# A value from two products, and a gate in one accumulation bank, in the last four blocks of a fused Fourier-mixing and ReGLU kernel

## The chip, the cores and the metric

One core of a Trainium2 chip. The metric is device time in microseconds of one execution of the whole program. A core has five engines with queues of their own: TensorE (PE in the profile, with its weight loads as PEld), VectorE (DVE), ScalarE (ACT), GpSimd (POOL) and SyncE (SP, which issues most transfers). Each takes its instructions in order and waits at each for what other engines must have done.

## The reference

```
X = fft(x, axis=1); X = fft(X, axis=2); y = X.real         # x: 8 x 3008 x 256
out = (max(y @ w_gate, 0) * (y @ w_val)) @ w_out           # weights 256 x 1536, 1536 x 256
```

There are 24064 rows (8 sequences of 3008). Inputs and output are float32; the kernel's products take bfloat16.

## The kernel before

The Fourier transform over the 256 channels is folded into the weights: `WA` holds the cosine-transformed and `WB` the sine-transformed gate (index 0) and value (index 1) weights. The transform over the sequence is done on PE from folded inputs and gives, for each sequence b, a cosine part `U` and a sine part `V`. Row j of the result and its mirror row S - j have the same cosine product and sine products of opposite sign. So a **tile**, which is 128 of the 1536 hidden features (`fi`, 0 to 11) by one **block** of columns (512, 512 or 481: `thirds`), gives two halves of the hidden layer `h`: one from cosine plus sine, one from cosine minus sine. `WM` is -2 times `WB`, with row 0 set to zero; row 0 of `V` carries one channel that has no sine, and its term is seeded into the bank separately: ACT writes `CB` times a column of `b2` into the bank (`seed`, L1011) before the products add to it.

After sequence 0, which is done in another way, there are 7 x 3 x 12 = 252 tiles, and the program makes one call of `slot` for each. A slot works on five tiles at once. For tile `cur` with number fi:

- `nxt` (two ahead): PE makes the sine product of the gate in bank `g` (`sine_part`, L1016), ACT copies it out (L1019); PE adds the cosine product to the seeded bank `p` (`cosine_part`, L1023); DVE forms the sum, `sp` (`both`, L1027), and POOL the difference, `sm` (L1028).
- `after` (three ahead): ACT seeds its bank `p`. There are two such banks.
- `pending` (one behind): PE adds `WM` times `V` to its value bank `v` (`mirror`, L879), which turns cosine plus sine into cosine minus sine; DVE multiplies it by the positive part of `sm` (`relu_mult` in `second`, L909).
- `cur`: PE makes the value's cosine and sine products (`value`, L873 and L874); DVE multiplies by the positive part of `sp` (L909).
- In two places of the slot PE runs `outs` products of 256 columns (L781), the last layer's output of the block before, 5/8 after the sine product and the rest at the end. After 24 of them a bank of output is full; ACT evicts it (L794, one eviction per slot from the list `evict`) and SP sends it to memory (L806).

For a 481-column tile SP also copies the last 66 columns of `h` to `LB` (`keep_rest`, L904). `sums` holds the DVE steps of the sequence's transform; POOL's folding of the next sequences' inputs is dealt out by `run_fold`. Both are done before the last block of sequence 6. The bank `d` belongs to the transform's products. `kvec` is used only for the tables of the transform, while sequence 0 is worked on.

The bank for each output and the order of everything on each engine are those of the program text; no planner moves them.

Of the kernel before, what the change touches and what calls it, by code (L numbers as in the profile page):

```python
# [12 lines left out]
BF16 = mybir.dt.bfloat16  # L13
# [16 lines left out]
def dram(ap, offset, pattern):  # L30
    return bass.AP(ap.tensor, offset, [list(p) for p in pattern])
# [3 lines left out]
def kernel(  # L35
# [27 lines left out]
    def single(name, shape, dt=F32, pool=const):  # L63
        return pool.tile(shape, dt, name=name, tag=name)
# [218 lines left out]
    ums = single("ums", [128, 1])  # L283
    m2 = single("m2", [128, 1])
    half_pi = single("half_pi", [128, 1])
    kvec = single("kvec", [128, NK])
    dvec = single("dvec", [128, 129], pool=st_)
    go = single("go", [128, 2])
    c128p = single("c128p", [128, 2, 3, 2])
# [212 lines left out]
            nc.gpsimd.tensor_tensor(FF[0][p, 0, t, :, 0:1], even[:, :, 0:1], even[:, :, 0:1], op=ALU.add)  # L502
    start_pool.__exit__(None, None, None)
    ch128 = nc.dram_tensor("ch128", (B, 4 * NJ + 1), BF16, kind="Internal").ap()
    b2 = single("b2", [128, NF])
    wrow = nc.dram_tensor("wrow", (1, DF), BF16, kind="Internal").ap()
    brow = single("brow", [128, NF], BF16)


    def even_table(n, c):  # L510
# [321 lines left out]
    for seg in (2, 3):  # L832
        more.setdefault((1, 8 + seg), []).append(lambda seg=seg: minus_v(nc.scalar, seg))

    more[(1, 1)].append(lambda: nc.sync.dma_start(out=wrow, in_=WB[0][0:1, :]))
    more[(1, 4)].append(lambda: nc.sync.dma_start(out=brow[:], in_=dram(wrow, 0, [[1, 128], [128, NF]]), allow_slow_non_contiguous=True))
    more[(2, 2)] = [lambda: nc.scalar.copy(b2[:], brow[:])]
    more_1 = {}
    for at, step in zip((-5, -4, -3, -2, -1, 7, 7, 8, 14, 17), channel_loads() + channel_turn()):
# [16 lines left out]
    def run_one(todo):  # L856
        if todo:
            todo.pop(0)()
# [62 lines left out]
    def value(st):  # L921
        st["v"] = bank("v")
        two(st["v"], st, 1)
# [63 lines left out]

    def new_tiles():  # L990
        for b in range(1, B):
            for blk, block in enumerate(thirds):
                for fi in range(NF):
                    st = tile_of(block, fi, uv[b])
                    st["b"] = b
                    st["kind"] = "o" if (b, blk, fi) == (1, 0, 6) else "n"
                    st["lead"] = (b, blk, fi) == (1, 0, 0)
                    yield st

# [21 lines left out]
    def cosine_part(st):  # L1021
        n = st["n"]
        nc.tensor.matmul(st["p"][:, 0:n], lhsT=WA[0][:, st["f"]], rhs=st["us"], start=False, stop=True, skip_group_check=True)  # L1023

    def both(st):
        n, (q, sp, sm) = st["n"], st["s"]
        nc.vector.scalar_tensor_tensor(sp[:, 0:n], in0=q[:, 0:n], scalar=-0.5, in1=st["p"][:, 0:n], op0=ALU.mult, op1=ALU.add)  # L1027
        nc.gpsimd.tensor_tensor(sm[:, 0:n], sp[:, 0:n], q[:, 0:n], op=ALU.add)  # L1028

    def slot(cur, mid, nxt, after, outs, fold_us):  # L1030

        stop = len(todo_out)

        def out(part):
            run(todo_out, len(todo_out) - stop + outs * part // 8)
        old = nxt is not None and nxt["kind"] == "o"
        new = nxt is not None and not old
# [36 lines left out]
        return cur  # L1074
# [4 lines left out]
    for b in range(B):  # L1079
# [4 lines left out]
        for blk, block in enumerate(blocks):  # L1084
# [44 lines left out]
            if (b, blk) == (0, 0):  # L1129
                for fi in range(NF):  # L1130
                    st = tile_of(block, fi, (U, V, CB))
                    add_h(st, hs)
                    if fi == 8:
                        todo_out = out_steps(b, block, hs, True)
                    pending = first_tile(st, more.get((0, fi), ()), 6)
                mirror(pending["g"], pending, 0)
                relu(pending)
            elif not paired:
                for fi in range(NF):
                    st = tile_of(block, fi, (U, V, CB))  # L1140
                    add_h(st, hs)
                    tag = {(3, 8): "g", (3, 9): "d", (3, 10): "g", (3, 11): "d"}.get((blk, fi), "p")
                    last = []
                    if (blk, fi) == (3, 11):
                        last = [lambda: (sine_part(ahead[1]), cosine_part(ahead[1]), both(ahead[1]), seed(ahead[2]))]
                    if (blk, fi) == (3, 9):
                        ahead = [next(tiles) for _ in range(3)]
                        more[(3, 9)] += [lambda: seed(ahead[0], prime())]
                        more[(3, 10)] += [lambda: seed(ahead[1], prime())]
                        more[(3, 11)] += [lambda: (sine_part(ahead[0]), cosine_part(ahead[0]), both(ahead[0]))]  # L1150
                    if (blk, fi) == (1, 8):
                        run(todo_out, len(todo_out))
                        todo_out = out_steps(b, block, hs, True)
                    pending = single_tile(st, 3 if blk == 1 else per_tile // 2, more_b.get((blk, fi), ()), last, tag)
                    run(todo_dft, DFT_0[blk - 1][fi])
            else:
                for fi in range(NF):
                    at = NF * blk + fi
                    cur = ahead.pop(0)
                    add_h(cur, hs)  # L1160
                    ahead.append(next(tiles, None))
                    outs = per_tile
                    if (b, blk) == (B - 1, 2) and fi > 8:
                        outs = (10, 11, 17)[fi - 9]
# [52 lines left out]
```

## Time and profile before

| | |
|---|---|
| time, median of 3 runs | 629.87 us (629.80 to 630.07) |
| the profiled execution's own time | 629.88 us |
| its span, first to last instruction | 628.1 us |
| DVE, ACT, POOL busy | 88%, 71%, 80% of the span |
| POOL busy in 400 to 450 us, and in 560 to 580 us | 44.66 of 50 us, 13.19 of 20 us |
| granted PE clock | 1.00 |

A line of the groups view reads: source line, engine, operation, output and input by the program's names, shapes, count, then busy time and mean duration, then the engine's idle time ahead of these instructions and what ended most of it. A line of the timeline reads: start in us, duration, engine, line, operation, names, shapes, count of merged instructions, and in brackets the idle time ahead of it with its releaser. A line of the windows view gives a stretch, its length, then busy time and instruction count of PE, PEld, DVE, ACT and POOL, the granted clock, the DMA engines' share and their GB/s. Matmuls are pipelined, and the ends of their rows are modelled.

### The profile page before, as it was taken

What the parts mean: (1) busy time and instruction counts of PE and PEld (TensorE: products, weight loads), DVE (VectorE), ACT (ScalarE), POOL (GpSimd) and SP (SyncE); (2) the same over time, 40 slices, a digit from 0 to 9 for tenths busy, and PEclk for the clock granted to TensorE, in tenths of its full rate; (3) what the DMA queues carried; (4) which work ended last, traced back from release to release, by engine and by line L of the source; (5) the groups of instructions that cost most, each with busy time, mean ns of one, the idle gap of its engine ahead of it and who ended that gap; (6) DMA issues with size and microseconds to landing.
All of it is one profiled execution on the core that took longest, in us unless ns stands there. A gap on an engine that the chain in (4) does not pass through costs nothing.

```text
span 628.1 us, 12374 instructions
## 1 busy us (share of the span) xinstructions
PE 617.9 (98%) x4057; PEld 398.2 (63%) x4102; DVE 550.9 (88%) x979; ACT 445.8 (71%) x814; POOL 502.7 (80%) x478
## 2 busy tenths in 40 slices
PE   8999999999999999999999999999999999999997
PEld 3566666666666666666666666666666666666666
DVE  8886676999899899988999999899999989999991
ACT  7796667777677767777777767777777777777762
POOL 8988992998899988799979989699886566666660
PEclk9999999999999999999999999999999999999999
DMA  9954758734263427315362326211221111211113
GB/s 240 210 201 130 169 184 106 186 66 141 86 155 137 132 70 196 101 48 161 91 185 68 131 76 138 61 52 35 76 62 37 42 60 56 60 35 50 53 50 95
DMA packets 84465, 66.47 MB, mean 106 GB/s; under 512 B 40070, under 2 KB 67494, under 8 KB 84400
## 3 DMA queue, kind: packets, MB, share of 16 engines
q1 hardware_dynamic: 79814, 60.01, 34.5%
q0 software_dynamic: 3984, 4.92, 4.0%
q8 instruction: 32, 0.52, 0.4%
q10 hardware_dynamic: 602, 0.75, 0.3%
q14 instruction: 33, 0.27, 0.1%
HBM read 41.88 MB, written 34.17 MB: 121 GB/s over the span
## 4 chain that ended last, share of the span: by engine, by line
PE 93%; DVE 3%; issue 1%; ACT 1%; DMA 1%; DVEq 0%; ACTq 0%
PE o L781 37%; PE v L874 10%; PE v L879 10%; PE g L1016 8%; PE p L1023 8%; PE v L873 8%; PE d L585 4%; DVE h L909 2%; PE p L879 1%; PE p L873 1%; PE p L874 1%; PE v L395 1%; DMA XG<-in_x_dram 1%; DVE h L898 1%; DVE r L1027 1%
## 5 line engine op out<-in xcount | busy, mean ns | idle before, releaser
L1028 POOL TENSOR_TENSOR r<-r 128x512 f32<-128x512 f32 (+1 forms) x251 | 312.8, 1252 | 100.0 <-DVE r L1027 98.9
L909 DVE SCALAR_TENSOR_TENSOR h<-r,v 128x512 bf16<-128x512 f32 (+1 forms) x502 | 317.3, 673 | 39.1 <-PE v L879 25.5
L781 PE MATMUL o<-wo,h 128*128 128x256 bf16 x2172 | 330.7, 273 | 0.0
L781 PEld LDWEIGHTS <-h 128*128 128x128 bf16 x2220 | 216.4, 97 | 112.7 <-issue 1.6
L1011 ACT ACTIVATE p<-CB,b 128x512 f32<-128x512 bf16 (+1 forms) x251 | 171.7, 684 | 73.5 <-DVE r L1027 72.6
L1019 ACT COPY r<-g 128x512 f32<-128x512 f32 (+1 forms) x251 | 144.8, 577 | 65.4 <-PE g L1016 56.8
L1027 DVE SCALAR_TENSOR_TENSOR r<-r,p 128x512 f32<-128x512 f32 (+1 forms) x251 | 168.1, 670 | 0.6 <-ACT r L1019 0.6
L874 PE MATMUL v<-V,WB 128*128 128x512 bf16 (+3 forms) x296 | 108.7, 367 | 2.2
L879 PE MATMUL v<-V,WM 128*128 128x512 bf16 (+1 forms) x252 | 94.4, 375 | 1.1 <-DVE h L909 0.7
L1016 PE MATMUL g<-V,WM 128*128 128x512 bf16 (+1 forms) x251 | 94.2, 375 | 0.2
L1023 PE MATMUL p<-U,WA 128*128 128x512 bf16 (+1 forms) x251 | 94.2, 375 | 0.0
L873 PE MATMUL v<-U,WA 128*128 128x512 bf16 (+3 forms) x254 | 92.7, 365 | 0.0
L898 DVE TENSOR_TENSOR h<-r,v 128x376 bf16<-128x376 f32 (+2 forms) x90 | 46.0, 546 | 17.3 <-PE v L879 9.1
L873 PEld LDWEIGHTS <-WA 128*128 128x128 bf16 x348 | 33.9, 97 | 39.9 <-issue 10.7
L874 PEld LDWEIGHTS <-WB 128*128 128x128 bf16 x348 | 33.9, 97 | 33.7 <-ACT WB L677 0.2
L794 ACT COPY os<-o 128x512 f32<-128x512 f32 x92 | 52.6, 571 | 3.5 <-issue 3.0
L198 POOL TENSOR_TENSOR XG<-XG,XD 128x510 f32<-128x510 f32 x42 | 52.9, 1267 | 0.6 <-DMA XG<-xr 0.6
L889 ACT ACTIVATE r<-p 128x376 f32<-128x376 f32 (+1 forms) x80 | 38.0, 486 | 17.8 <-PE p L879 9.6
L206 POOL TENSOR_TENSOR AA<-XG 128x510 f32<-128x510 f32 x42 | 45.3, 1089 | 0.0
L1016 PEld LDWEIGHTS <-WM 128*128 128x128 bf16 x251 | 24.5, 98 | 5.7 <-issue 0.3
L879 PEld LDWEIGHTS <-WM 128*128 128x128 bf16 x253 | 24.7, 98 | 3.1
L1023 PEld LDWEIGHTS <-WA 128*128 128x128 bf16 x251 | 24.5, 98 | 3.3 <-issue 0.2
(183 smaller groups left out, 412.4 us busy)
## 6 DMA issues: line engine op xcount, KB each, us to landing
out_dram<-os SPq DMA_DIRECT2D x124, 128.0 KB
xr<-in_x_dram SPq DMA_DIRECT2D x12, 768.0 KB
XG<-xr SPq DMA_DIRECT2D x12, 768.0 KB
XD<-in_x_dram SPq DMA_DIRECT2D x15, 512.0 KB
out_dram<-os SPq DMA_DIRECT2D x35, 112.0 KB
XD<-in_x_dram SPq DMA_DIRECT2D x8, 448.0 KB
CB<-ch SPq DMA_DIRECT2D x7, 376.2 KB
out_dram<-os SPq DMA_DIRECT2D x13, 96.0 KB
```

Of the source, the lines that this page charges most:

```text
L198: e.tensor_tensor(XG[p, r, t, ::-1, 1:D], XG[p, r, t, ::-1, 1:D], XD[p, r, t, :, D - 1:0:-1], op=ALU.add)
L781: nc.tensor.matmul(st["p"][0:m, q, :], lhsT=lhs(f), rhs=wo[:, f, :], start=(f == 0 and not (early and q)), stop=(f == NF - 1), skip_group_ ...
L873: nc.tensor.matmul(bank[:, 0:st["n"]], lhsT=WA[i][:, st["f"]], rhs=st["us"], start=True, stop=False)
L874: nc.tensor.matmul(bank[:, 0:st["n"]], lhsT=WB[i][:, st["f"]], rhs=st["vs"], start=False, stop=True)
L879: nc.tensor.matmul(bank[:, 0:st["n"]], lhsT=W[i][:, st["f"]], rhs=v, start=False, stop=True, skip_group_check=True)
L909: nc.vector.scalar_tensor_tensor(half_h(st, sign), in0=st["s"][1 + sign][:, 0:n], scalar=0.0, in1=st["v"][:, 0:n], op0=ALU.max, op1=ALU.mult)
L1011: nc.scalar.activation(st["p"][:, 0:st["n"]], st["c"], ACTF.Copy, scale=b2[:, st["fi"]:st["fi"] + 1])
L1016: nc.tensor.matmul(st["g"][:, 0:n], lhsT=WM[0][:, st["f"]], rhs=st["vs"], start=True, stop=True)
L1019: nc.scalar.copy(q[:, 0:n], st["g"][:, 0:n])
L1023: nc.tensor.matmul(st["p"][:, 0:n], lhsT=WA[0][:, st["f"]], rhs=st["us"], start=False, stop=True, skip_group_check=True)
L1027: nc.vector.scalar_tensor_tensor(sp[:, 0:n], in0=q[:, 0:n], scalar=-0.5, in1=st["p"][:, 0:n], op0=ALU.mult, op1=ALU.add)
L1028: nc.gpsimd.tensor_tensor(sm[:, 0:n], sp[:, 0:n], q[:, 0:n], op=ALU.add)
```

## The change

In the four last blocks (the third of sequence 6 and all of sequence 7), two kinds of tiles are worked in another way. The block is named by (sequence, third), as in (7, 0).

- Tiles 3 and 8 (`SHORT`): the value's bank is `d`, seeded by ACT two slots ahead. PE adds the cosine product a slot ahead, ACT keeps twice that in SBUF (`a`), POOL takes the positive part of `sm`. In its own slot PE adds one sine product from `WV`, a copy of `WB[1]` with row 0 zero; DVE makes the first half as before, then `a` minus the bank, and POOL multiplies that by `sm` for the second half. The third product (`mirror`) and the second `relu_mult` are gone for these tiles. In `slot`, `both` of a later tile stands ahead of the difference.
- Tile 5 (`JOINED`): the gate has one bank. After the cosine product ACT keeps twice the bank (`sm`); in the next slot PE adds the sine product to the same bank, ACT copies it out as `sp`, and POOL subtracts it from `sm`. `sine_part` and `both` are gone for this tile. The slot in which its cosine product is made takes two more output products and no eviction; the next takes two fewer.
- Once: `WV` is made by three ACT multiplications in sequence 2 in the space of `kvec`; the seeds' table `b2` and its load have 24 columns instead of 12; row 0 of `WB[0]` is overwritten by zeros in sequence 5; one product opens bank `d` at the start of (6, 2).

```diff
-    kvec = single("kvec", [128, NK])
+    kvec = single("kvec", [128, DF // 2])
...
-    b2 = single("b2", [128, NF])
+    b2 = single("b2", [128, 2 * NF])
+    WV = kvec[:].bitcast(BF16)
...
-    more[(1, 1)].append(lambda: nc.sync.dma_start(out=wrow, in_=WB[0][0:1, :]))
-    more[(1, 4)].append(lambda: nc.sync.dma_start(out=brow[:], in_=dram(wrow, 0, [[1, 128], [128, NF]]), ...))
+    more[(1, 1)].append(lambda: [nc.sync.dma_start(out=wrow[i:i + 1], in_=WB[i][0:1, :]) for i in range(2)])
+    more[(1, 4)].append(lambda: nc.sync.dma_start(out=brow[:], in_=dram(wrow, 0, [[1, 128], [128, 2 * NF]]), ...))
...
+    JOINED, SHORT = (5,), (3, 8)
...
+                    late = b == 7 or (b, blk) == (6, 2)
+                    st["kind"] = "o" if (b, blk, fi) == (1, 0, 6) else "j" if late and fi in JOINED else "n"
+                    st["short"] = late and fi in SHORT
...
+    def copy_cosine(st):
+        n, sp, sm = st["n"], space(), space()
+        st["s"] = sm, sp, sm
+        nc.scalar.mul(sm[:, 0:n], st["p"][:, 0:n], 2.0)
+
+    def add_sine(st):
+        n, (_, sp, sm) = st["n"], st["s"]
+        nc.tensor.matmul(st["p"][:, 0:n], lhsT=WB[0][:, st["f"]], rhs=st["vs"], start=False, stop=True, ...)
+        nc.scalar.copy(sp[:, 0:n], st["p"][:, 0:n])
+        nc.gpsimd.tensor_tensor(sm[:, 0:n], sm[:, 0:n], sp[:, 0:n], op=ALU.subtract)
+
+    def open_bank():
+        p = bank("d")
+        nc.tensor.matmul(p[:], lhsT=WA[1][:, 0:128], rhs=U[:, 0:512], start=True, stop=True)
+
+    def seed_value(st):
+        st["v"] = bank("d")
+        nc.scalar.activation(st["v"][:, 0:st["n"]], st["c"], ACTF.Copy, scale=b2[:, NF + st["fi"]:NF + st["fi"] + 1])
+
+    def value_cosine(st):
+        n, st["a"], sm = st["n"], space(), st["s"][2][:, 0:st["n"]]
+        nc.tensor.matmul(st["v"][:, 0:n], lhsT=WA[1][:, st["f"]], rhs=st["us"], start=False, stop=True, ...)
+        nc.scalar.mul(st["a"][:, 0:n], st["v"][:, 0:n], 2.0)
+        nc.gpsimd.tensor_scalar(sm, sm, scalar1=0.0, op0=ALU.max, scalar2=None)
+
+    def value_sine(st):
+        n = st["n"]
+        nc.tensor.matmul(st["v"][:, 0:n], lhsT=WV[:, st["f"]], rhs=st["vs"], start=False, stop=True, ...)
+
+    def value_second(st):
+        n = st["n"]
+        a = st["a"][:, 0:n]
+        nc.vector.tensor_tensor(a, a, st["v"][:, 0:n], op=ALU.subtract)
+        nc.gpsimd.tensor_tensor(half_h(st, 1), st["s"][2][:, 0:n], a, op=ALU.mult)
+        if n == 481:
+            keep_rest(st)
...
     def slot(cur, mid, nxt, after, outs, fold_us):
+        joined, ready = (st is not None and st["kind"] == "j" for st in (nxt, mid))
+        outs += 2 * joined - 2 * ready
...
+        if ready:
+            add_sine(mid)
-        if new and not lead:
+        if (new or joined) and not lead:
             cosine_part(nxt)
+        if joined:
+            copy_cosine(nxt)
         if not lead:
             seed(after)
-        if pending is not None:
+        if mid is not None and mid["short"]:
+            value_cosine(mid)
+        if pending is not None and not pending.get("short"):
             mirror(pending["v"], pending, 1)
-        if pending is not None:
             second(pending)
-        value(cur)
+        if cur["short"]:
+            value_sine(cur)
+        else:
+            value(cur)
...
+        if cur["short"]:
+            value_second(cur)
+        if nxt is not None and nxt["short"]:
+            seed_value(nxt)
         run_fold(fold_us)
-        run_one(evict)
+        if not joined:
+            run_one(evict)
...
+                    if (b, at) in ((2, 5), (2, 9), (2, 13)):
+                        f = slice(128 * (at - 5), 128 * (at - 1))
+                        nc.scalar.mul(WV[:, f], WM[1][:, f], -0.5)
+                    if (b, at) == (5, 0):
+                        nc.sync.dma_start(out=WB[0][0:1, :], in_=WM[0][0:1, :])
+                    if (b, at) == (6, 24):
+                        open_bank()
```

More of the change, by code (lines that the diff above doesn't have):

```diff
@@ L504 @@
     ch128 = nc.dram_tensor("ch128", (B, 4 * NJ + 1), BF16, kind="Internal").ap()
-    b2 = single("b2", [128, NF])
-    wrow = nc.dram_tensor("wrow", (1, DF), BF16, kind="Internal").ap()
-    brow = single("brow", [128, NF], BF16)
+    b2 = single("b2", [128, 2 * NF])
+    WV = kvec[:].bitcast(BF16)
+    wrow = nc.dram_tensor("wrow", (2, DF), BF16, kind="Internal").ap()
+    brow = single("brow", [128, 2 * NF], BF16)
     def even_table(n, c):
@@ L833 @@
         more.setdefault((1, 8 + seg), []).append(lambda seg=seg: minus_v(nc.scalar, seg))
-    more[(1, 1)].append(lambda: nc.sync.dma_start(out=wrow, in_=WB[0][0:1, :]))
-    more[(1, 4)].append(lambda: nc.sync.dma_start(out=brow[:], in_=dram(wrow, 0, [[1, 128], [128, NF]]), allow_slow_non_contiguous=True))
+    more[(1, 1)].append(lambda: [nc.sync.dma_start(out=wrow[i:i + 1], in_=WB[i][0:1, :]) for i in range(2)])
+    more[(1, 4)].append(lambda: nc.sync.dma_start(out=brow[:], in_=dram(wrow, 0, [[1, 128], [128, 2 * NF]]), allow_slow_non_contiguous=True))
     more[(2, 2)] = [lambda: nc.scalar.copy(b2[:], brow[:])]
@@ L995, in new_tiles @@
                     st["b"] = b
-                    st["kind"] = "o" if (b, blk, fi) == (1, 0, 6) else "n"
+                    late = b == 7 or (b, blk) == (6, 2)
+                    st["kind"] = "o" if (b, blk, fi) == (1, 0, 6) else "j" if late and fi in JOINED else "n"
+                    st["short"] = late and fi in SHORT
                     st["lead"] = (b, blk, fi) == (1, 0, 0)
@@ L1028, in both @@
         nc.gpsimd.tensor_tensor(sm[:, 0:n], sp[:, 0:n], q[:, 0:n], op=ALU.add)
+    def copy_cosine(st):
[4 more added lines that the diff above has]
+        n, (_, sp, sm) = st["n"], st["s"]
+        nc.tensor.matmul(st["p"][:, 0:n], lhsT=WB[0][:, st["f"]], rhs=st["vs"], start=False, stop=True, skip_group_check=True)
+        nc.scalar.copy(sp[:, 0:n], st["p"][:, 0:n])
[8 more added lines that the diff above has]
+        n, st["a"], sm = st["n"], space(), st["s"][2][:, 0:st["n"]]
+        nc.tensor.matmul(st["v"][:, 0:n], lhsT=WA[1][:, st["f"]], rhs=st["us"], start=False, stop=True, skip_group_check=True)
+        nc.scalar.mul(st["a"][:, 0:n], st["v"][:, 0:n], 2.0)
+        nc.gpsimd.tensor_scalar(sm, sm, scalar1=0.0, op0=ALU.max, scalar2=None)
+    def value_sine(st):
+        n = st["n"]
+        nc.tensor.matmul(st["v"][:, 0:n], lhsT=WV[:, st["f"]], rhs=st["vs"], start=False, stop=True, skip_group_check=True)
+    def value_second(st):
[5 more added lines that the diff above has]
+            keep_rest(st)
     def slot(cur, mid, nxt, after, outs, fold_us):
+        joined, ready = (st is not None and st["kind"] == "j" for st in (nxt, mid))
+        outs += 2 * joined - 2 * ready
         stop = len(todo_out)
@@ L1036, in slot @@
         old = nxt is not None and nxt["kind"] == "o"
-        new = nxt is not None and not old
+        new = nxt is not None and nxt["kind"] == "n"
         if old:
```

## The prediction, made before the changed kernel ran

> **What bounds the kernel now.** I read the page's span and busy times first, then busy time by stretches of the span, then who waited for whom, then the timeline of one slot, engine by engine. "Slot" is one call of `slot`: one tile's value and one later tile's gate.
>
> ```profile
> span 628.1 us, 12374 instructions
> PE 617.9 (98%) x4057; PEld 398.2 (63%) x4102; DVE 550.9 (88%) x979; ACT 445.8 (71%) x814; POOL 502.7 (80%) x478
> ```
> ```profile
> 560.00:580.00 20.00, 19.85 (x133) 13.03 (x134) 19.30 (x32) 14.23 (x24) 13.19 (x11) 1.00 0.15 48
> ```
>
> PE is busy for 98% of the span, and for 19.85 of 20 us in a stretch inside the last four blocks; DVE, at 19.30, is hardly less loaded. A busy PE alone proves little, since a matmul's row includes its drain. So I asked for PE's waits from 525 to 601 us, nearly all of the stage that changes. The answer is its header, with no row under it:
>
> ```profile
> engine line waited for: us in total, times, longest us
> ```
>
> PE waits for nobody there. What counts then is the distance from one product's start to the next:
>
> ```profile
> 562.01 0.38 PE L1016 MATMUL g<-V,WM 128*128 128x512 bf16 x1
> 562.23 0.71 PE L781 MATMUL o<-wo,h 128*128 128x256 bf16 x5
> 562.77 0.38 PE L1023 MATMUL p<-U,WA 128*128 128x512 bf16 x1
> 562.99 0.38 PE L879 MATMUL v<-V,WM 128*128 128x512 bf16 x1
> 563.20 0.38 PE L873 MATMUL v<-U,WA 128*128 128x512 bf16 x1
> 563.42 0.38 PE L874 MATMUL v<-V,WB 128*128 128x512 bf16 x1
> 563.63 0.49 PE L781 MATMUL o<-wo,h 128*128 128x256 bf16 x3
> 563.96 0.38 PE L1016 MATMUL g<-V,WM 128*128 128x512 bf16 x1
> ```
>
> This is a slot of a 512-column block. It repeats after 563.96 - 562.01 = 1.95 us. Between 562.77 and 563.63 lie four products of 512 columns, (563.63 - 562.77) / 4 = 0.215 us each, though each row lasts 0.38; an output product of 256 columns takes (562.77 - 562.23) / 5 = 0.108. Five times 0.215 and eight times 0.108 make 1.94: the slot is the sum of PE's spacings. The same in a block of 481 columns:
>
> ```profile
> 600.71 0.37 PE L1016 MATMUL g<-V,WM 128*128 128x481 bf16 x1
> 601.46 0.37 PE L1023 MATMUL p<-U,WA 128*128 128x481 bf16 x1
> 601.66 0.37 PE L879 MATMUL v<-V,WM 128*128 128x481 bf16 x1
> 602.07 0.37 PE L874 MATMUL v<-V,WB 128*128 128x481 bf16 x1
> 602.60 0.37 PE L1016 MATMUL g<-V,WM 128*128 128x481 bf16 x1
> ```
>
> The slot is 602.60 - 600.71 = 1.89 us, a product (602.07 - 601.46) / 3 = 0.203.
>
> Now DVE, which could take over:
>
> ```profile
> 562.72 0.68 DVE L1027 SCALAR_TENSOR_TENSOR r<-r,p 128x512 f32<-128x512 f32 x1
> 563.47 1.28 DVE L909 SCALAR_TENSOR_TENSOR h<-r,v 128x512 bf16<-128x512 f32 x2
> 564.68 0.68 DVE L1027 SCALAR_TENSOR_TENSOR r<-r,p 128x512 f32<-128x512 f32 x1
> ```
> ```profile
> 602.14 1.22 DVE L909 SCALAR_TENSOR_TENSOR h<-r,v 128x481 bf16<-128x481 f32 x2
> 603.27 0.65 DVE L1027 SCALAR_TENSOR_TENSOR r<-r,p 128x481 f32<-128x481 f32 x1
> ```
>
> L909 twice and L1027 once are its work in a slot. Two L909 rows last 1.28 together, yet L1027 starts 564.68 - 563.47 = 1.21 after the first: operations start 0.605 apart, (603.27 - 602.14) / 2 = 0.565 at 481 columns. Three of them need 1.815 of 1.95 us. DVE keeps 0.135 us in reserve per slot, and no more.
>
> **The change, part by part.** All of it is set against the profiled execution, 629.88 us (span 628.1 and 1.78 around it), which is 0.01 from the median of the three runs, 629.87.
>
> *PE.* A short tile's value was three products (L873, L874, and L879 in the next slot). It becomes two: the cosine product a slot earlier and a sine product in place of L873 and L874. One product is gone for each short tile. Tiles 3 and 8 of four blocks are eight: four at 0.215 and four at 0.203, 1.67 us. `open_bank` adds one product of 0.215. A joined gate has two products as before; its sine product moves one slot on, and two output products (2 x 0.108) fill the place it leaves, to be missed in the next slot, so PE's sum stays. Net -1.67 + 0.215 = -1.46 us, if PE waits for nothing new. It is not the 0.38 of a row times eight: rows overlap. At one place the Trainium skill differs: the page "TensorE: Matmul & The Clock Gate", section "Back-to-back issue gap", gives about 131 ns per 512-column product in a stream of loads and products. By that the net would be 7 x 0.131 = 0.92; the 0.215 here speaks against it (the same section's 216 ns for an isolated product agrees).
>
> *DVE.* Costs of its new operation and of what the other engines are given come from these groups, or their nearest relatives:
>
> ```profile
> L898 DVE TENSOR_TENSOR h<-r,v 128x512 bf16<-128x512 f32 x2 | 1.4, 684 | 0.3 <-PE v L879 0.3
> L1028 POOL TENSOR_TENSOR r<-r 128x512 f32<-128x512 f32 x167 | 212.0, 1274 | 72.7 <-DVE r L1027 72.0
> L487 POOL TENSOR_SCALAR AA<-AA 128x377 f32<-128x377 f32 x6 | 3.8, 627 | 0.5
> L1011 ACT ACTIVATE p<-CB,b 128x512 f32<-128x512 bf16 x167 | 115.8, 693 | 47.2 <-DVE r L1027 46.2 <-PE v L874 0.6 <-PE p L1003 0.4
> L1019 ACT COPY r<-g 128x512 f32<-128x512 f32 x167 | 97.7, 585 | 47.7 <-PE g L1016 39.3 <-POOL r L1028 6.0 <-POOL AA L206 0.4
> ```
>
> A joined gate takes L1027 off DVE in one slot. For a short tile the second L909 goes and `value_second`'s difference comes; the nearest row is the 512-column TENSOR_TENSOR that also reads PSUM, 684 ns, like L909's 0.68. So per short tile DVE saves nothing, but the work moves a slot ahead. At tile 3 this is free: the same slot has the joined gate, so three operations stay. At tile 8 there are four in one slot: tile 7's second half, tile 8's first half, tile 10's L1027 and the difference. What waits behind the fourth? The next slot's first operation, L909 of tile 9; and behind that PE, because tile 9's third product (L879) adds into the bank that this L909 reads. What such a release costs is seen at the end of the program:
>
> ```profile
> 614.17 1.23 DVE L909 SCALAR_TENSOR_TENSOR h<-r,v 128x481 bf16<-128x481 f32 x2 [1.39 <-PE v L874]
> ```
> ```profile
> 615.45 0.36 PE L879 MATMUL v<-V,WM 128*128 128x481 bf16 x1 [0.58 <-DVE h L909]
> ```
>
> DVE ends at 614.17 + 1.23 = 615.40 and PE starts at 615.45, so 0.05. Counted from the start of tile 8's slot, at 512 columns: L879 issues at 562.99 - 562.01 = 0.98 and DVE starts at 563.47 - 562.01 = 1.46. Four starts 0.605 apart free DVE at 3.88. Tile 9's L909 runs to 3.88 + 0.68 = 4.56, and PE may go on at 4.61. PE, whose slots 8 and 9 are both one product shorter (1.735), wants L879 of tile 9 at 2 x 1.735 + 0.98 = 4.45. It waits 0.16. At 481 columns: 1.43 + 4 x 0.565 = 3.69, with 0.65 and 0.05 4.39, against 2 x 1.687 + 0.95 = 4.32, so 0.07; in the last block slots 9 and 10 carry more output products, and nothing waits. Together 2 x 0.16 + 0.07 = 0.39 us. The bounds: 0 if DVE turns round a little faster than 0.605, and, if each operation held DVE for its full 0.68 (0.65), 4.18 + 0.68 + 0.05 - 4.45 = 0.46 twice and 0.43 once, 1.35. I take 0.39, from spacings seen in this very stage. Net: -1.46 + 0.39 = -1.07.
>
> *ACT.* Its slot, with an eviction in it:
>
> ```profile
> 562.48 0.59 ACT L1019 COPY r<-g 128x512 f32<-128x512 f32 x1 [0.30 <-PE g L1016]
> 563.44 0.69 ACT L1011 ACTIVATE p<-CB,b 128x512 f32<-128x512 bf16 x1 [0.37 <-DVE r L1027]
> 564.07 0.57 ACT L794 COPY os<-o 128x512 f32<-128x512 f32 x1
> 564.55 0.58 ACT L1019 COPY r<-g 128x512 f32<-128x512 f32 x1
> ```
>
> Copies start 564.55 - 564.07 = 0.48 apart, a seed holds ACT for 564.07 - 563.44 = 0.63. A short tile adds a seed (0.63) and a scaled copy (nearest row L1019, 585 ns, so 0.48), a joined gate one copy more. The narrow place is the slot after a joined gate. There `add_sine` issues after one product and three output products, at 0.215 + 3 x 0.108 = 0.54; a product's result reaches ACT 562.48 - 562.01 = 0.47 later, at 1.01; the copy ends at 1.59; the next seed, which needs that bank, starts 0.04 later (L1027 ends at 562.72 + 0.68 = 563.40, the seed starts at 563.44) and ends at 1.63 + 0.69 = 2.32. Its cosine product is due at 1.735 + 0.76 = 2.495 (562.77 - 562.01). The cover is 0.17 us, so the cost is nothing, and every ACT operation that lands ahead of that seed uncovers 0.48 - 0.17 = 0.31. The eviction that would stand there is held back by `if not joined`, to the end of this slot; the output bank it empties is wanted again only two groups of 24 products later.
>
> *POOL.* Per short tile it adds an elementwise maximum (nearest 0.627 for 377 elements, so about 0.85 for 512; between 0.63 and 1.27) and the product for the mirrored half (nearest 1.27). Around tile 8 it has 4 x 1.27 + 0.85 = 5.93 in three slots of 1.95 + 0.215 + 1.735 + 1.735 = 5.64, so it falls 0.3 behind. That is hidden: the product is read by the next block's output products, the sums two slots later. On SP the copy of a 481-column tile's rest waits for POOL now, some 1.3 us longer, and output transfers queue behind it; four output buffers cover that. If they did not, PE would wait up to 1.3 at each of four such tiles, no row points to that.
>
> *Early parts.* `brow` has 3072 elements to fetch, not 1536:
>
> ```profile
> 46.01 0.39 SPq L836 DMA_DIRECT2D brow<-wrow  x1
> ```
> ```profile
> 46.00:50.00 4.00, 4.00 (x29) 2.43 (x27) 3.08 (x8) 3.03 (x8) 0.76 (x2) 1.00 0.91 200
> 50.00:54.00 4.00, 4.00 (x29) 2.38 (x27) 2.17 (x5) 2.57 (x6) 4.00 (x5) 1.00 0.19 62
> ```
> ```profile
> 63.66 0.19 ACT L837 CAST b<-brow 128x12 f32<-128x12 bf16 x1
> ```
>
> The load, issued at 46.01, keeps the DMA engines at 0.91 up to 50 and leaves 0.19 after; as long again would end by 54, and the reader comes at 63.66. It costs nothing; with the cover gone, 4 us at most. The extra row copies are 3 KB each. The three `WV` multiplications (at most the seed's 0.69 each) stand ahead of a slot's copy on ACT in the third sequence:
>
> ```profile
> 188.44 0.58 ACT L794 COPY os<-o 128x512 f32<-128x512 f32 x1
> 188.91 0.58 ACT L1019 COPY r<-g 128x512 f32<-128x512 f32 x1
> 189.86 0.69 ACT L1011 ACTIVATE p<-CB,b 128x512 f32<-128x512 bf16 x1 [0.37 <-DVE r L1027]
> ```
>
> Here an eviction, a copy and a seed follow each other at 188.44, 188.91 and 189.86, with 0.37 idle before the seed; PE wants that seed's bank a further 0.59 after it ends (563.44 + 0.69 = 564.13 against 562.77 + 1.95 = 564.72). 0.37 + 0.59 is more than 0.69: nothing, and 3 x 0.69 = 2.1 if it is uncovered.
>
> **The rivals.**
> *All hidden.* DVE turns round fast enough for tile 9: -1.46, 628.4 us. For it: only 0.16 is missing. Against: the 0.605.
> *DVE takes the gain.* Each operation holds DVE for its full duration: stalls 1.35, net -0.11, 629.8 us. For it: 96% busy. Against: starts 0.605 apart. On the Trainium skill's page "VectorE: DVE Perf Modes", section "The DRAIN you can't avoid", the next operation does not start before the pipe empties unless it is one that is not held; the trace shows the exception.
> *A product frees less than its spacing*, at least the 0.108 of the nearest shorter one: 7 x 0.108 = 0.76, with the stall 629.5 us. For it is only the page's 131 ns; against it the equal spacings.
> *ACT becomes the bound, and the kernel slower.* If the seed and copy for tile 3 (0.63 + 0.48) are still queued when the joined gate's copies come, 1.11 - 0.17 = 0.94 is lost at each of four gates: 629.88 - 1.07 + 3.76 = 632.6 us. It decides from a backlog of 0.17 + 1.07 / 4 = 0.44. For it: three additions fall into slots 1 to 4, 0.63 + 2 x 0.48 = 1.6. Against: ACT idles 0.30 and 0.37 in such slots, 2.7 in four, less one or two evictions.
> *The `WV` work is uncovered*: 628.8 + 2.1 = 630.9 us.
> That the change does not do what it says can't be: the products are counted out in the program.
>
> **How the numbers follow.** Forecast: 629.88 - 1.07 = 628.8 us. Chances: forecast 0.50, all hidden 0.20, DVE 0.12, frees less 0.03, ACT 0.12, `WV` 0.03. A measurement of this kernel tells about 0.2% (1.26 us) from no change. Faster by more needs stalls below 0.2: all hidden, and 0.15 of the forecast's 0.50, together 0.35. Slower is ACT and `WV`, 0.15. Within 0.2% is the rest, 0.50. The range: down to 628.2, all hidden less 0.2 for the scatter of the runs (629.8 to 630.07); up to 630.2, which takes in the DVE case and a part of the ACT backlog, and leaves out ACT in full and `WV`, 0.15.
>
> **What would show it.** L879 should appear 8 times less often. Slots 8 and 9 should last 1.735 and 1.69 us. PE should wait for L909 before tile 9's L879, some 0.16 us in (7, 0) and (7, 1). No PE wait on ACT's seed should appear. A PE row waiting for L1011 at slots 4 and 5 proves the ACT rival; waits of 0.4 and more at tile 9 prove the DVE one; slots 8 and 9 shortened by less than 0.2 without a wait prove the third; a gap on PE near slots 5, 9 and 13 of the third sequence proves `WV`. Late `brow` would show as idle ACT before its copy.

## The result, and the profile after

| | before | after |
|---|---|---|
| median, 14 runs each | 629.88 us (629.59 to 630.53) | 628.42 us (628.22 to 628.99) |
| ratio | | 0.9978 (95% interval 0.997 to 0.9985) |
| span of the profiled execution | 628.1 us | 626.4 us |

1.46 us faster, 0.22%. A second comparison of the same two kernels on another chip gave 629.99 and 628.69 us, ratio 0.998 (0.9971 to 0.9989).

First the page's span and busy times, the stretch from 560 to 580 us, and PE's waits from 515 to 616 us, each of the changed kernel:

```profile
span 626.4 us, 12435 instructions
PE 618.8 (99%) x4095; PEld 397.7 (63%) x4095; DVE 547.7 (87%) x975; ACT 455.6 (73%) x837; POOL 523.4 (84%) x494
```
```profile
560.00:580.00 20.00, 20.00 (x136) 13.10 (x135) 19.01 (x31) 16.16 (x28) 17.76 (x15) 1.00 0.16 49
```
```profile
PE v L880 <- DVE h L910: 0.2, 1, 0.2
```

The columns of the stretch are PE, PEld, DVE, ACT and POOL. DVE fell from 19.30 to 19.01 us in it, ACT rose from 14.23 to 16.16 and POOL from 13.19 to 17.76. PE is full, 20.00. The 19.85 of before was no idle time: in that stretch three products of L873 have a weight load and no row of their own. For the same reason the count of PE's rows grows, from 4057 to 4095, though the weight loads fall from 4102 to 4095: eight products gone and one added. Behind 515 us the third product has 44 rows (L880), where it had 52 (L879). The view of waits knows one wait in the whole stage; waits shorter than a row's overlap with the next (about 0.16 us) do not show in it, so PE has to be read from start to start.

PE in the timeline, the slot of tile 3 in (7, 0), from one L1028 (the cosine product, L1023 before) to the next L1021 (L1016 before):

```profile
550.81 0.38 PE L1028 MATMUL p<-U,WA 128*128 128x512 bf16 x1
551.02 0.38 PE L880 MATMUL v<-V,WM 128*128 128x512 bf16 x1
551.24 0.38 PE L1064 MATMUL d<-V,kvec 128*128 128x512 bf16 x1
551.46 0.60 PE L782 MATMUL o<-wo,h 128*128 128x256 bf16 x4
551.89 0.38 PE L1021 MATMUL g<-V,WM 128*128 128x512 bf16 x1
```

Tile 3's value is the one product L1064, at the spacing of 0.215: this slot lost exactly one product. The slots of tiles 8 and 9 last 1.74 us each, from L1028 to L1028, and 1.69 at 481 columns, where they had 1.95 and 1.89.

Then the wait that was forecast, in (7, 0): DVE in the slot of tile 8, and PE ahead of tile 9's third product (L880):

```profile
561.77 0.68 DVE L910 SCALAR_TENSOR_TENSOR h<-r,d 128x512 bf16<-128x512 f32 x1
562.37 0.68 DVE L1032 SCALAR_TENSOR_TENSOR r<-r,p 128x512 f32<-128x512 f32 x1
562.96 0.68 DVE L1069 TENSOR_TENSOR r<-r,d 128x512 f32<-128x512 f32 x1
563.56 0.68 DVE L910 SCALAR_TENSOR_TENSOR h<-r,v 128x512 bf16<-128x512 f32 x1
```
```profile
563.93 0.38 PE L1028 MATMUL p<-U,WA 128*128 128x512 bf16 x1
564.30 0.38 PE L880 MATMUL v<-V,WM 128*128 128x512 bf16 x1
564.51 0.38 PE L874 MATMUL v<-U,WA 128*128 128x512 bf16 x1
```

Tile 8's first half, tile 10's sum, the difference and tile 9's first half start 0.60, 0.59 and 0.60 apart. The last ends at 563.56 + 0.68 = 564.24; L880 starts at 564.30, where 563.93 + 0.215 = 564.15 would have followed without a wait: 0.15 us.

And the last slot, whose rows of before are in the prediction: PE's products for tiles 10 and 11 (L880), and DVE.

```profile
612.11 0.37 PE L880 MATMUL v<-V,WM 128*128 128x481 bf16 x1
613.86 0.36 PE L880 MATMUL v<-V,WM 128*128 128x481 bf16 x1 [0.21 <-DVE h L910]
```
```profile
612.58 1.23 DVE L910 SCALAR_TENSOR_TENSOR h<-r,v 128x481 bf16<-128x481 f32 x2 [1.02 <-PE v L880]
```

The pair of L910 starts 612.58 - 612.11 = 0.47 us after tile 10's product. In the kernel before, tile 10's product was this row:

```profile
613.33 0.37 PE L879 MATMUL v<-V,WM 128*128 128x481 bf16 x1
```

It started at 613.33 and the pair at 614.17, 0.84 later. So PE now waits 0.37 us less ahead of tile 11's last product, at a place that the change does not touch.

Distances between PE starts, less the spacing of the product in front, give all of PE's waits from 516 to 616 us:

| | before | after |
|---|---|---|
| slot of tile 0 of (6, 2), ahead of L880 (L879 before) | 0.10 | 0 |
| ahead of tile 9's L880 (L879 before), in (6, 2), (7, 0), (7, 1), (7, 2) | 0, 0, 0, 0.05 | 0.05, 0.15, 0.17, 0.16 |
| ahead of tile 11's last product | 0.75 | 0.38 |
| sum | 0.90 | 0.91 |

The eight products, less the one that opens the bank, are 1.67 - 0.215 = 1.46 us. The new waits and the lost ones cancel. From tile 11's cosine product in (6, 1), at 516.55 and 516.43 us, to the end of the span are 111.57 us before and 109.98 after: 1.59 less, of which 0.12 is the landing of the last transfer.

### The profile page after: what moved, and what is told of

It is laid out like the page before. It is cut to its first block, busy times and chain, and to the rows that moved or that the text cites. A ratio compares the mean times of both kernels' runs of the same rounds, so it can differ in the third digit from the quotient of the medians.

```text
span 626.4 us, 12435 instructions
## 1 busy us (share of the span) xinstructions
PE 618.8 (99%) x4095; PEld 397.7 (63%) x4095; DVE 547.7 (87%) x975; ACT 455.6 (73%) x837; POOL 523.4 (84%) x494
## 4 chain that ended last, share of the span: by engine, by line
PE 93%; DVE 3%; ACT 1%; issue 1%; DMA 1%; DVEq 0%; ACTq 0%
PE o L782 37%; PE v L880 10%; PE v L875 9%; PE v L874 9%; PE g L1021 8%; PE p L1028 8%; PE d L586 4%; DVE h L910 2%; PE p L880 1%; PE p L874 1%; PE p L875 1%; PE v L395 1%; DMA XG<-in_x_dram 1%; DVE h L899 1%; DVE r L1032 1%
## 5 line engine op out<-in xcount | busy, mean ns | idle before, releaser
L1033 POOL TENSOR_TENSOR r<-r 128x512 f32<-128x512 f32 (+1 forms) x247 | 308.0, 1254 | 77.7 <-DVE r L1032 76.3
L910 DVE SCALAR_TENSOR_TENSOR h<-r,v 128x512 bf16<-128x512 f32 (+1 forms) x486 | 307.8, 673 | 40.6 <-PE v L880 30.0
L1016 ACT ACTIVATE p<-CB,b 128x512 f32<-128x512 bf16 (+1 forms) x251 | 171.8, 685 | 66.9 <-DVE r L1032 65.2
L1024 ACT COPY r<-g 128x512 f32<-128x512 f32 (+1 forms) x247 | 142.6, 577 | 58.3 <-PE g L1021 49.3
L1032 DVE SCALAR_TENSOR_TENSOR r<-r,p 128x512 f32<-128x512 f32 (+1 forms) x247 | 165.2, 669 | 0.6 <-ACT r L1024 0.6
L875 PE MATMUL v<-V,WB 128*128 128x512 bf16 (+3 forms) x288 | 105.6, 367 | 0.0
L874 PE MATMUL v<-U,WA 128*128 128x512 bf16 (+3 forms) x288 | 105.6, 367 | 0.0
L1028 PE MATMUL p<-U,WA 128*128 128x512 bf16 (+1 forms) x251 | 94.1, 375 | 0.0
L1021 PE MATMUL g<-V,WM 128*128 128x512 bf16 (+1 forms) x247 | 92.6, 375 | 0.2
L880 PE MATMUL v<-V,WM 128*128 128x512 bf16 (+1 forms) x244 | 91.4, 375 | 0.7 <-DVE h L910 0.4
L795 ACT COPY os<-o 128x512 f32<-128x512 f32 x92 | 52.6, 571 | 3.4 <-PE o L782 3.4
L1021 PEld LDWEIGHTS <-WM 128*128 128x128 bf16 x247 | 24.2, 98 | 5.6 <-issue 0.3
L1028 PEld LDWEIGHTS <-WA 128*128 128x128 bf16 x251 | 24.6, 98 | 3.3 <-issue 0.2
L880 PEld LDWEIGHTS <-WM 128*128 128x128 bf16 x245 | 24.0, 98 | 3.8
```

Source lines behind the costliest of these rows:

```text
L874: nc.tensor.matmul(bank[:, 0:st["n"]], lhsT=WA[i][:, st["f"]], rhs=st["us"], start=True, stop=False)
L875: nc.tensor.matmul(bank[:, 0:st["n"]], lhsT=WB[i][:, st["f"]], rhs=st["vs"], start=False, stop=True)
L880: nc.tensor.matmul(bank[:, 0:st["n"]], lhsT=W[i][:, st["f"]], rhs=v, start=False, stop=True, skip_group_check=True)
L910: nc.vector.scalar_tensor_tensor(half_h(st, sign), in0=st["s"][1 + sign][:, 0:n], scalar=0.0, in1=st["v"][:, 0:n], op0=ALU.max, op1=ALU.mult)
L1016: nc.scalar.activation(st["p"][:, 0:st["n"]], st["c"], ACTF.Copy, scale=b2[:, st["fi"]:st["fi"] + 1])
L1021: nc.tensor.matmul(st["g"][:, 0:n], lhsT=WM[0][:, st["f"]], rhs=st["vs"], start=True, stop=True)
```

## The experiments

The column "stage" goes from tile 11's cosine product in (6, 1) to the end of the span, because executions reach that product at different times (516.41 to 516.83 us, and 517.85 in one); PE's waits are summed as above, up to 616 us.

| kernel | median us | before, same chip | ratio (95%) | stage us | PE waits |
|---|---|---|---|---|---|
| before | 629.88 | | | 111.57 | 0.90 |
| the change | 628.42 | 629.88 | 0.9978 (0.997 to 0.9985) | 109.98 | 0.91 |
| the change again | 628.69 | 629.99 | 0.998 (0.9971 to 0.9989) | 109.99 | |
| joined gates 5 and 10 | 628.42 | 630.04 | 0.9975 (0.9966 to 0.9984) | 109.48 | 0.38 |
| the same again | 628.55 | 629.99 | 0.9976 (0.9967 to 0.9985) | 109.48 | |
| short tiles only | 629.12 | 630.04 | 0.9988 (0.9979 to 0.9997) | 110.65 | 1.57 |
| eviction at once | 630.01 | 630.04 | 1.0001 (0.9992 to 1.001) | 111.25 | 2.18 |
| difference first | 629.69 | 630.04 | 0.9995 (0.9986 to 1.0004) | 111.00 | 1.92 |
| first three blocks | 629.01 | 629.99 | 0.9984 (0.9975 to 0.9993) | 110.28 | 0.80 |
| before again | 631.22 | one run | | 111.58 | |
| before, 4 DVE memsets | 629.56 | 629.95 | 0.9992 (0.9983 to 1.0001) | 111.22 | 0.53 |
| change, 12 DVE memsets | 628.97 | 629.95 | 0.9983 (0.9974 to 0.9992) | 110.36 | 1.27 |
| joined gates only | 629.90 | 629.95 | 1.0 (0.9991 to 1.0009) | 111.45 | 0.53 |

**A second joined gate, tile 10.** It takes tile 10's sum out of the slot of tile 8, where DVE has four operations.

```diff
-    JOINED, SHORT = (5,), (3, 8)
+    JOINED, SHORT = (5, 10), (3, 8)
```

> The change with a second joined gate, tile 10, beside the short tile 8. Theory (PE's spacing sets the time, and what the change leaves on the table is DVE's fourth operation in the slot of tile 8): that slot then has three DVE operations, PE's wait ahead of tile 10's value, 0.15 to 0.16 us in two blocks and 0.05 in a third, is gone, and the time is 0.35 below the change, 628.05 us. Rival (that wait is no real loss, the whole 1.46 is PE's): no difference, 628.4. Rival (ACT is at its limit round a joined gate): three or four more gates that lose 0.3 each, 629.3.

DVE in the slot of tile 8, and PE at tile 9's third product, in (7, 0):

```profile
561.76 0.68 DVE L910 SCALAR_TENSOR_TENSOR h<-r,d 128x512 bf16<-128x512 f32 x1
562.36 0.68 DVE L1069 TENSOR_TENSOR r<-r,d 128x512 f32<-128x512 f32 x1
563.15 0.69 DVE L910 SCALAR_TENSOR_TENSOR h<-r,v 128x512 bf16<-128x512 f32 x1
```
```profile
564.04 0.38 PE L1028 MATMUL p<-U,WA 128*128 128x512 bf16 x1
564.25 0.38 PE L880 MATMUL v<-V,WM 128*128 128x512 bf16 x1
```

Tile 9's first half starts at 563.15, not 563.56, and L880 0.21 after L1028: the wait is gone. It is gone in all four blocks, and the stage is 0.50 us shorter, about the 0.53 by which PE's waits fell. So the waits ahead of tile 9's third product in the change are real losses, and their cause is DVE's fourth operation. ACT lost nothing at the further gates. In device time the two kernels, run together the second time, are 628.55 and 628.69 with overlapping intervals; this experiment's faster stage is shown by the traces, not by the clock of the whole.

> The changed kernel once more, beside the run with two joined gates, on one chip. Theory: 1.4 to 1.5 us under the kernel before, and the same stretches of the trace as in its first profile, the waits at tile 10 included.

The change's trace came out the same (stage 109.99). Its time is 1.30 under the kernel before, a little less than the 1.4 to 1.5 that were expected, and its ratio is within the first interval.

> Joined gates at tiles 5 and 10 once more, beside the change on the same chip. Theory (its trace has no wait at tile 10): 0.35 to 0.5 us under the change. Rival (another wait outside the last four blocks takes it back): the same time as the change.

The stage is 109.48 again, the time 0.14 under the change, not 0.35 to 0.5: this profiled execution reached the stage at 516.83, 0.39 later than the change's. Where executions lose time ahead of the stage was not followed.

**Short tiles only.**

```diff
-    JOINED, SHORT = (5,), (3, 8)
+    JOINED, SHORT = (), (3, 8)
```

> The change without joined gates: short tiles 3 and 8 alone. Theory (DVE's fourth operation): now the slot of tile 3 has four operations as well, so PE waits ahead of tile 5's value too, about 0.16 twice and 0.06 twice, 628.9 us, and the trace has waits of L910 there. Rival (DVE's queue does not matter): as the change, 628.4. If the eight products did not bring the gain but the joined gates did: near 629.9.

PE waits ahead of tile 4's third product now too, 0.08, 0.15, 0.15 and 0.08 us, in the slot of tile 5, as at tile 9, together 0.46, and the gain in the median falls from 1.46 to 0.92. The stage is 0.67 longer than the change's, so these waits are two thirds of it. The rest is one more wait, which no theory had, 0.23 us ahead of tile 10's third product in (7, 0), on DVE and on PE:

```profile
564.58 0.68 DVE L1032 SCALAR_TENSOR_TENSOR r<-r,p 128x512 f32<-128x512 f32 x1
565.56 1.29 DVE L910 SCALAR_TENSOR_TENSOR h<-r,v 128x512 bf16<-128x512 f32 x2 [0.29 <-PE v L875]
```
```profile
566.46 0.38 PE L1028 MATMUL p<-U,WA 128*128 128x512 bf16 x1
566.90 0.38 PE L880 MATMUL v<-V,WM 128*128 128x512 bf16 x1
```

L910 starts 565.56 - 564.58 = 0.98 after L1032, while its product had been ready; PE's L880 then comes 566.90 - 566.46 = 0.44 after L1028, not 0.215. The experiments on the last slot, further down, explain it: the semaphore record ahead of that L910 is number 1470.

**Eviction at once.**

```diff
-        if not joined:
-            run_one(evict)
+        run_one(evict)
```

> The change, with the eviction not held back in the slot of a joined gate. Theory (ACT's cover in the slot after the gate is 0.17 us, one more operation of 0.48 uncovers 0.31): PE waits for the seed, four times about 0.3, 629.6 us. Rival (ACT idles enough to take it): 628.4. If ACT is worse off than counted, because two seeds slip: 4 x 0.6, 630.8.

ACT round the joined gate in (7, 0), in this kernel, and PE behind it; then ACT in the change:

```profile
552.69 0.59 ACT L795 COPY os<-o 128x512 f32<-128x512 f32 x1
553.16 0.59 ACT L1024 COPY r<-g 128x512 f32<-128x512 f32 x1
553.64 0.61 ACT L1044 COPY r<-p 128x512 f32<-128x512 f32 x1
554.28 0.69 ACT L1016 ACTIVATE p<-CB,b 128x512 f32<-128x512 bf16 x1
```
```profile
555.02 0.38 PE L1028 MATMUL p<-U,WA 128*128 128x512 bf16 x1 [0.17 <-ACT p L1016]
```
```profile
552.87 0.59 ACT L1044 COPY r<-p 128x512 f32<-128x512 f32 x1
553.49 0.69 ACT L1016 ACTIVATE p<-CB,b 128x512 f32<-128x512 bf16 x1
554.12 0.58 ACT L795 COPY os<-o 128x512 f32<-128x512 f32 x1
```

With the eviction (L795) in front, the gate's second copy (L1044) starts at 553.64 and the seed at 554.28; PE waits for the seed 0.31, 0.33, 0.34 and 0.31 us in the four blocks, 0.31 each by the forecast. The stage is 1.27 longer than the change's, and the time does not differ from that of the kernel before. It is 630.01, 0.4 over the forecast; 0.16 of that is this chip, where the kernel before took 630.04 and not 629.88. The eviction's place is worth nearly as much as the products.

**Difference first.**

```diff
-        if new:
-            both(nxt)
-...
-        if cur["short"]:
-            value_second(cur)
+        if cur["short"]:
+            value_second(cur)
+        if new:
+            both(nxt)
```

> The change, with the value's difference ahead of the later tile's sum on DVE. Theory (queue order on DVE): only tile 8 has both in one slot; the sum of tile 10 ends 0.6 later, the seed that needs its bank ends 0.46 after tile 12's cosine product is due (0.36 at 481 columns), in place of the 0.16 (0.05) lost at tile 10: 0.3 more in each of three blocks, 629.3 us. Rival (the same work in another order is the same time): 628.4.

DVE in the slot of tile 8, the seed on ACT, and PE at tile 12's cosine product, in (7, 0):

```profile
562.39 0.68 DVE L910 SCALAR_TENSOR_TENSOR h<-r,d 128x512 bf16<-128x512 f32 x1
562.99 0.68 DVE L1069 TENSOR_TENSOR r<-r,d 128x512 f32<-128x512 f32 x1
563.59 0.68 DVE L1032 SCALAR_TENSOR_TENSOR r<-r,p 128x512 f32<-128x512 f32 x1
```
```profile
564.31 0.69 ACT L1016 ACTIVATE p<-CB,b 128x512 f32<-128x512 bf16 x1 [1.19 <-DVE r L1032]
```
```profile
565.05 0.38 PE L1028 MATMUL p<-U,WA 128*128 128x512 bf16 x1 [0.33 <-ACT p L1016]
```

The sum (L1032) starts at 563.59, where in the change it started at 562.37; the seed waits for its end, 564.27, and PE waits 0.42, 0.49 and 0.48 us in three blocks, in place of the change's 0.05, 0.15 and 0.17. Stage 1.02 longer; 0.9 was forecast. Which of two DVE operations goes first decides two thirds of the gain in the stage, though DVE does the same work.

**The last slot.** Three kernels asked whether the 0.37 us at the end belong to the last block, to one execution, or to neither.

```diff
-                    late = b == 7 or (b, blk) == (6, 2)
+                    late = (b, blk) in ((6, 2), (7, 0), (7, 1))
```

> The change in (6, 2), (7, 0) and (7, 1) alone; (7, 2) is as in the kernel before. Two products of 0.203 come back: 0.41 us over the change. Besides, the profiles differ at the last slot: DVE's L909 for tile 10 starts 0.84 us after the product it waits for in the kernel before, 0.47 after it in the change and in every variant so far, and the program's end comes 0.37 earlier for it. Theory A (the last block's program makes that delay): it is back, 629.2 us. Theory B (a delay of that one profiled execution): 0.47 here, 628.8 us.

> The kernel before, profiled once more, for its last slot. Theory A (the program makes the delay): L909 for tile 10 starts 0.84 us after its product again. Theory B (one execution's delay): 0.47 after it, and a span 0.37 shorter than in the first profile, 627.75.

Both theories fell. The kernel before shows 0.844 us in its second profile as in its first: the program makes the delay. With the change in the first three blocks alone, the last block as before, it is 0.474: the last block does not make it. What differs is how many DVE records lie in front. A record is a line of DVE in the trace, semaphore waits included; they are counted from 0. Behind a semaphore wait with nothing running, DVE usually starts its next operation 0.07 us later. In the kernel before, 0.42 to 0.44 us pass behind the waits with the numbers 190, 446, 702, 1342 and 1598, which all lie multiples of 128 apart; numbers 446, 702 and 1342, at 169.70, 269.55 and 514.75 us, are late in the change too. At the other steps of 128, from number 62 on, DVE was running or the record was no such wait. In the kernels traced here, a wait of this kind whose number is 62 plus a multiple of 128 is late every time, and apart from the program's first 18 us no other shows more than 0.22 us. In the kernel before, with 1608 records, number 1598 is the semaphore wait ahead of the last slot's pair. The change has 1596 records and ends ahead of it. So two kernels moved the number and nothing else in the stage, by memsets of one column on DVE in sequence 0 (n = 4 in the kernel before, n = 12 in the change):

```diff
+    idle = single("idle", [128, 16])
...
+    more[(1, 7)] = more.get((1, 7), []) + [lambda: [nc.vector.memset(idle[:, k:k + 1], 0.0) for k in range(n)]]
```

> The kernel before, with four one-column memsets more on DVE in sequence 0, where DVE waits. Theory (DVE's instruction stream has a gap of about 0.37 us at every 128th record, at the records numbered 62, 190, ... 1598; in the kernel before, number 1598 is the semaphore record ahead of L909 in the last slot, with nothing running that would hide it): the last slot moves on to 1602, its L909 starts 0.47 after its product instead of 0.84, and the program ends 0.37 earlier, 629.5 us. Rival (the last slot's delay has to do with what the last blocks compute): 0.84 and 629.9 us.

> The change, with twelve such memsets. It has 12 DVE records fewer than the kernel before, so its last slot's semaphore record is number 1586. Theory: twelve more put it on 1598, the delay is there again, 0.84, and 0.37 us are lost, 628.9 us. Rival: 0.47 and no loss, 628.5 us.

Tile 10's product on PE and the pair on DVE, in the kernel before with four more, then in the change with twelve more:

```profile
613.28 0.37 PE L881 MATMUL v<-V,WM 128*128 128x481 bf16 x1
```
```profile
613.75 1.23 DVE L911 SCALAR_TENSOR_TENSOR h<-r,v 128x481 bf16<-128x481 f32 x2 [0.65 <-PE v L881]
```
```profile
612.43 0.37 PE L882 MATMUL v<-V,WM 128*128 128x481 bf16 x1
```
```profile
613.27 1.23 DVE L912 SCALAR_TENSOR_TENSOR h<-r,v 128x481 bf16<-128x481 f32 x2 [1.39 <-PE v L877]
```

613.75 - 613.28 = 0.47 and 613.27 - 612.43 = 0.84. Four instructions more shortened the stage of the kernel before by 0.35 us; its median is 0.39 lower, with an interval that just includes no change (0.9983 to 1.0001). Twelve more lengthened the change's stage by 0.38. The delay goes with the record's number, and 0.37 us of the change's gain in the stage come from its smaller count of DVE records and not from the products it removes. With the delay put back, the change with twelve more still gains 0.98 us in the time (629.95 to 628.97) and 1.21 in the stage: that much the delay does not explain.

**Joined gates only**, no short tiles and no opened bank:

```diff
-    JOINED, SHORT = (5,), (3, 8)
+    JOINED, SHORT = (5,), ()
...
-                    if (b, at) == (6, 24):
-                        open_bank()
```

> Joined gates at tile 5 alone, no short tiles, no opened bank: PE's sum is that of the kernel before. Theory: nothing gained in the slots; DVE has at least four records fewer, so the last slot leaves number 1598 and 0.37 us are gained at the end, 629.5 us. Rival (relieving DVE is worth something where PE has no waits): more than 0.5 us gained, with shorter slots near tile 5. Rival (joined gates cost ACT something by themselves): longer slots near tile 5.

The slots round tile 5 sum to what they were (1.85 and 2.06 for 1.95 twice), so joined gates alone gain and lose nothing. The pair in the last slot is on time, but the program is not 0.37 faster. DVE and PE behind it:

```profile
613.90 1.23 DVE L910 SCALAR_TENSOR_TENSOR h<-r,v 128x481 bf16<-128x481 f32 x2 [1.02 <-PE v L880]
616.02 0.66 DVE L910 SCALAR_TENSOR_TENSOR h<-r,v 128x481 bf16<-128x481 f32 x1 [0.89 <-PE o L782]
```
```profile
615.38 1.14 PE L782 MATMUL o<-wo,h 128*128 128x256 bf16 x9
616.74 0.28 PE L782 MATMUL o<-wo,h 128*128 128x256 bf16 x1 [0.21 <-DVE h L910]
```

With 1604 records, number 1598 is now the wait ahead of the very last L910: it starts 616.02 - 613.90 = 2.12 after the pair, in the change 614.33 - 612.58 = 1.75. PE's output products wait for it: the one at 616.74 starts 0.48 after the one ahead of it, where 0.11 is usual. So PE loses 0.37 again, behind 616 us and outside the column of waits; the stage keeps 0.12, in the landing of the last transfer. The time, 629.90, is that of the kernel before; the forecast of 629.5 had the gap only leaving its place, not where it would come down.

## Why the prediction was right, and where it was not

**The sum.** Forecast 628.8, measured 628.42, in the range 628.2 to 630.2. The forecast's mechanism held: PE's spacing sets the time, the removed products are worth 0.215 and 0.203 each and not 0.38, the opened bank costs 0.215 less a wait of 0.10 in its own slot, which is there in every kernel without the opened bank and in none with it. The gain of 1.46 is the number of the rival "all hidden", and yet that rival is wrong: the forecast waits are there. Right total, wrong account.

**DVE's fourth operation.** Forecast 0.16, 0.16, 0.07 and none for (7, 0), (7, 1), (6, 2) and (7, 2); measured 0.15, 0.17, 0.05 and 0.16. The step that failed is "in the last block slots 9 and 10 carry more output products, and nothing waits". Slot 10 there has no gate left to make (tile 12 does not exist), so ten output products, 1.09 us, stand between tile 9's value and its third product, where in (6, 2) and (7, 0) eight of them and two products of 0.215 stand, 1.30. PE comes to that product sooner, not later. The term is 0.53 instead of 0.39. The experiments with a second joined gate and without any show its cause. "DVE takes the gain" is refuted: starts are 0.60 apart, also behind the new TENSOR_TENSOR.

**What the account lacked.** 0.37 us at the end of the program, from a record's number, and 0.15 from two small waits that the kernel before had in the slot of tile 0 of (6, 2) and ahead of tile 9's third product in (7, 2), 0.10 and 0.05. None of them shows in the rows of a single ordinary slot. The 0.37 could have been read from the kernel before: its last slot's DVE pair started 0.84 behind its product, where 1.46 - 0.98 = 0.48 is what the prediction used. The prediction even quoted that row, for the release at its end.

The 0.37 is nearly the whole distance from 628.8 to 628.42. That the rest of the sum fits is in part luck: the waits at tile 9 were 0.14 more than forecast, and the two small waits that went took back 0.15. Where the change keeps the delay (twelve more memsets), PE's waits are 1.27 for 0.90, which is 0.37 more, beside the forecast 0.39.

**ACT.** The cover of 0.17 and the 0.31 per uncovered operation held to 0.03 us, as the eviction at once shows. The rival "ACT becomes the bound" was wrong for the change and right for that variant, though at 0.31 per gate and not 0.94. What it charged for, by the groups from 520 to 615 us:

```profile
L1060 POOL TENSOR_SCALAR r<-r 128x512 f32<-128x512 f32 x4 | 6.0, 1489 | 0.4
L1070 POOL TENSOR_TENSOR h<-r 128x512 bf16<-128x512 f32 x4 | 5.1, 1279 | 0.1
L1054 ACT ACTIVATE d<-CB,b 128x512 f32<-128x512 bf16 x4 | 2.7, 672 | 0.0
L1059 ACT ACTIVATE r<-d 128x512 f32<-128x512 f32 x4 | 2.3, 583 | 0.0
L1069 DVE TENSOR_TENSOR r<-r,d 128x512 f32<-128x512 f32 x4 | 2.7, 679 | 0.0
```

A seed of 672 ns, a scaled copy of 583 and the difference of 679 are close to what the nearest rows gave (693, 585 and 684). POOL's maximum is not: 1489 ns, where 0.85 was taken and 1.27 was the upper bound. The estimate and its bound failed together; nothing came of it, and all of PE's waits in the table above have other causes.

**Early parts.** The three `WV` multiplications and the cast of `b2`, as groups and as instructions of the tile `brow`:

```profile
L1230 ACT ACTIVATE kvec<-WM 128x512 bf16<-128x512 bf16 x3 | 1.9, 626 | 0.0
```
```profile
L838 ACT CAST b<-brow x1: 203/203/203, 63.6 to 63.6; 128x24 f32<-128x24 bf16 x1
```

626 ns each, between 188.8 and 205.8 us. PE's waits of 0.1 us and more from 180 to 215 us are the same in both kernels, 0.19, 0.21, 0.19 and 0.10 at the same products: the multiplications are hidden. The cast reads its table at 63.6 us as before.

**By pages of the Trainium skill.** The 131 ns per product of 512 columns of "TensorE: Matmul & The Clock Gate", section "Back-to-back issue gap", do not hold in this stream: the removed products gave 0.215 us each. The rule in "VectorE: DVE Perf Modes", section "The DRAIN you can't avoid", applies here only with its exception: four operations of 0.68 us start 0.60 apart.

## What to carry to other kernels

Where PE has no waits, cost an edit by the distance from start to start, and then follow each shared engine's queue slot by slot: an operation moved one slot, or one eviction left in place, here takes back as much as a product gives. A gain of a few tenths of a microsecond can come from where a record falls in an engine's instruction stream; look at places that the edit does not touch, and shift the stream by a few instructions that do nothing before such a gain is credited to the edit. A joined gate beside every short tile is the better version by the trace (0.50 us in the stage), though device time did not tell the two apart.

## What the runs showed of the hardware

- In these kernels, behind a semaphore wait whose record number is 62 plus a multiple of 128, DVE's next operation starts after 0.42 to 0.44 us, not after 0.07: about 0.35 more. It is hidden when an operation is running, and costs up to 0.37 us where DVE waits on the path that sets the end, or 0.23 in a loaded slot (short tiles only). The cause is open. A reload of instructions is suggested by the regularity, and by the profile's queue of kind "instruction", 33 packets of 8 KB in the kernel before: behind each of the five late starts there, one begins 1.08 to 1.76 us after the wait's record. By then the late operation has begun, so it is not this packet that DVE waited for.
- On GpSimd, a maximum of one 128x512 float32 tensor with a scalar took 1489 ns, longer than adding or multiplying two such tensors (1274 and 1279 ns). The profile gives the ends of this engine's rows only roughly; the starts say the same, 1.46 us from a maximum to the next row and 1.23 from a product (L1070).
